# A mixture-of-experts tail: the first expert's weights fetched ahead of its rows, hooks regrouped, and branch bodies moved, on one Trainium2 core

## The chip, the core and the metric

One core of a Trainium2 chip runs the whole program. The metric is the device time of one launch in microseconds; lower is better.

## What is computed

The reference has three stages on 4608 tokens (8 batches of 576) with 512 features:

```python
attn = softmax(q @ k_p.T * scale) @ v_p
x = ((x @ w1) * (x @ w2)) @ w3 @ w_out
logits = x @ w_gate + modality_bias[modality_id]
e_idx = argmax(logits)
out = gate * (relu(x @ ew1[e_idx]) @ ew2[e_idx])
```

`k_p` and `v_p` are keys and values pooled by 8 along the sequence. `w1`, `w2` are 512x1024, `w3` is 1024x1024, `w_out` 1024x512. There are 8 experts of 512x1024 and 1024x512, and each token goes to one of them. With this data only two experts get tokens: one 2330, the other 2278.

## The kernel before

Every fp32 product of the heavy part is made of three matmuls of fp32r halves: high·high, high·low and low·high (`mm3`, lines 114 to 116). So each fp32 operand exists as a high half, written by ScalarE (ACT), and a low half, the difference, written by VectorE (DVE). In tile names `h` and `l` (`xh`, `xl`; `abh`, `abl`) stand for them.

The tokens go through attention and the first MLP in nine chunks of 512. In a chunk `mm1` runs eight blocks `m` (24 matmuls of 128x512 for a and b, whose product is split to `abh[m]`, `abl[m]`), and `mm_w` multiplies that with the folded `w3 @ w_out` in four tiles of 128 tokens (24 matmuls each). DVE then makes the gate's logits of each tile (line 579, eight reductions), `routing` (lines 585 to 603) the gate value and the one-hot choice `r_oh`, and `place` (lines 606 to 626) each token's place in its expert's list: two small matmuls on PE count tokens (`rps`, lines 610 and 611), twelve DVE operations make addresses, GpSimd (POOL) scatters the token numbers to `lst` in DRAM.

The last chunk and all expert work stand in `experts` (line 684). There the order of each engine is the written order (`manual_schedule`); side work is put between matmul blocks by *hooks*: lists of functions that run behind block `m` of `mm1` or `emm1`, or behind tile `i` of `mm_w`. An engine does its instructions in this order, so one that waits holds up all that stands behind it on that engine.

- **mm1 of the last chunk, hooks `h1`.** Behind block 2, `place_all` of chunk 7, `first_expert` (which expert has most tokens so far), `first_loads`, and `take_raw2`. `first_loads` reads the expert's number into an SP register, waits until the scatters are done (`settle`, line 629), fetches the first 512 token numbers (`fetch_ids`, 705), gathers their rows on POOL (`gather`, 709, into `xg`) and starts four loads of raw `w1` (713); `take_raw2` starts four of raw `w2`. The raw weights are split into halves by `w1p` and `w2p` (`piece`, 715: high on ACT in line 719, low on DVE in 720) behind blocks 5, 6 and 7.
- **Between mm1 and mm_w**, `turn` (737) copies the 16-bit halves of the gathered rows apart (742, 743) and transposes them by DMA on SP (744) into `xTu`. `join` (746), in two parts behind tile 1 of `mm_w`, puts them together again (752, 753) and splits them (`xh` 754 on ACT, `xl` 755 on DVE).
- **First group** (925): `emm1` is eight blocks of 12 matmuls on the 512 gathered tokens. Each block's result goes through ReLU to `hT` (763 on ACT, 764 on DVE). Its results take four PSUM banks in turn, so block 4 starts only when lines 763 and 764 of block 0 are done. Hooks: `routing` of the last chunk behind block 0, `place_all` behind 3, `plan` (lines 856 to 907, some 40 small DVE operations that make the table of all later groups) behind 4, the last two pieces of `w2` behind 6 and 7. Then `emm2`: per tile of 128 tokens 24 matmuls with `w2`, scale, and scatter to `out`.
- **Later groups** (`group`, 947): seven groups of four tiles, one of three, one of two. Each prefetches the next group's rows and weights, and splits its own `w2` pieces behind the blocks of `emm1`; the turn of the next rows comes behind block 6, the join behind an early tile of `emm2`.
- **Branches**: groups stand nested in `tc.If go{n}_{g}` (line 976), n = 0 for four tiles, 1 for three, and in the outer `tc.If` per kind (988); the two-tile kind has an if with an else (981). Every engine runs them by itself. With this data the three-tile chain ends after its first group, so `go1_0` is false. A false block waits for the engine's own instructions and branches to the code behind the if. In the program before, all seven bodies of the chain stand right behind their compares, the false blocks behind them, next to the outer if of the two-tile kind.

The ring and the split:

```python
def mm_ps(name, shape=(P, 512)):
    return psum.tile(list(shape), F32, name=name, tag="mm", bufs=4)

nc.scalar.copy(h2, r)
(sub or nc.vector).tensor_tensor(l2, r, h2.bitcast(F32), op=ALU.subtract)
```

Of the kernel before, what the change touches and what calls it, by code (L numbers as in the profile page):

```python
# [22 lines left out]
P = 128  # L23
# [66 lines left out]
def _program(outer, tc, nc, I, out):  # L90
# [16 lines left out]
    def st4(name, shape, dtype):  # L107
        return st.tile(list(shape), dtype, name=name, tag="st4", bufs=6)
# [519 lines left out]
    def settle(ent):  # L628
        nc.sync.dma_start(ent[0:1], I["pads"][0:4].rearrange("(o a) b -> o a b", o=1))
# [54 lines left out]
    def experts(x, old):  # L684
# [16 lines left out]
        def load_reg(ap, hi, engines=(ET.SP,)):  # L701
            return nc.values_load(ap, engines=list(engines), min_val=0, max_val=hi, skip_runtime_bounds_check_because="bounded by construction")
# [9 lines left out]
        def load_e(src, er, m2, raw):  # L712
            nc.sync.dma_start(raw, src[ds(er, P), 1024 * m2:1024 * m2 + 1024])
# [88 lines left out]

        def first_loads():
            first["e"], s0r = load_reg(t0i[0:1, 0:1], 896), load_reg(t0i[0:1, 1:2], LIST - CAP)
            settle(ents[-1])
            fetch_ids(s0r, 4)
            xg2 = [st4("xg", (P, 2, 512), F32) for i in range(2)]
            xg.extend(xg2[i // 2][:, i % 2] for i in range(4))
            gather(xg, 4, (NC_ - 1) * 512)
            first["raw"] = [st4("raw", (P, 1024), F32) for _ in range(4)]  # L810
            for m2 in range(4):
                load_e(I["ew1"], first["e"], m2, first["raw"][m2])

        raw2, xT = [], []

# [20 lines left out]
        w2p = lambda *ms: lambda: pieces(raw2, w2e, ms)  # L836
        for f in late_logits(ch - 1, old):
            f()
        h1 = {0: [lambda: r7.append(routing(ch - 1, lg))], 2: [lambda: place_all(r7[0]), first_expert, first_loads, take_raw2],
              5: [lambda: [take(m) for m in range(2, 6)], w1p(0, 1)], 6: [w1p(2, 3, 4, 5)], 7: [lambda: take(6), w1p(6, 7), w2p(0, 1, 2, 3)]}  # L840
        ab = mm1(ch, x, h1)

        xTu = w12.tile([P, 8, 512], U16, name="xTu", tag=w_tag(7), bufs=1)
        turn(xg, 4, nc.scalar.copy)
        xT.extend(xp.tile([P, 4, 512], F32R, name=n, tag=n) for n in ("xh", "xl"))
        x2s = []
        lo = lambda i, es=range(E): logits(ch, i, x2s, es)
        hw = {i: [lambda i=i: lo(i)] for i in range(4)}
        hw[0].insert(0, w2p(4, 5))
        hw[1] = [lambda: join(xT, 4, nc.scalar.copy, (0,)), lambda: lo(1, range(4)), lambda: join(xT, 4, nc.scalar.copy, (2,)), lambda: lo(1, range(4, 8))]  # L850
        mm_w(ch, ab, hw, W, x2s)

# [71 lines left out]

        def first_group():
            r8, nr = [], []
            hooks = {0: [lambda: r8.append(routing(ch, lg))], 3: [lambda: place_all(r8[0])], 4: [plan], 6: [w2p(6)], 7: [w2p(7)]}
            emm1(xT, hT, 4, hooks)
            er, sr = regs(0, 0)
            settle(ents[-1])  # L930
            fetch_ids(sr, 4)
            emm2(hT, 0)
            gather(xg, 4)
            loads1(er, (0, 1))
            nc.sync.dma_start(fence, xg[3][0:1, 0:1])
            loads1(er, (2, 3))
            loads2(er)
            emm2(hT, 1)
            pieces(raw1, w1e, (0, 1))
            emm2(hT, 2)  # L940
            transposes(xT, xg, 4)
            pieces(raw1, w1e, range(2, 8))
            emm2(hT, 3)
# [3 lines left out]
        def group(nxt, tiles, ntiles):  # L947
            nr = nxt()
            if nr:
                loads1(nr[0])  # L950
            hooks = {m: [lambda m=m: pieces(raw2, w2e, (m,))] for m in range(8)}
            if nr:
                hooks[6] += [lambda: turn(xg, ntiles, nc.vector.tensor_copy)]
                hooks[IDC_M] += [lambda: fetch_ids(nr[1], ntiles), lambda: gather(xg, ntiles)]
                hooks[7] += [lambda: loads2(nr[0])]
            emm1(xT, hT, tiles, hooks)
            half = (tiles + 1) // 2
            for i in range(tiles):
                emm2(hT, i)
                if nr:  # L960
                    if i == half - 1:
                        join(xT, ntiles, nc.vector.tensor_copy)
                    pieces(raw1, w1e, PIECES[tiles][i])

# [4 lines left out]
        def chain(n, g, tiles):  # L969

            if n < 2:
                if g < NG[n] - 2:
                    tc.mark_branch_hint_location(f"go{n}_{g}", counts[n] > g + 1, allE)
                group(lambda: regs(n, g + 1), tiles, tiles)
                if g < NG[n] - 2:
                    with tc.If(counts[n] > g + 1, label=f"go{n}_{g}"):  # L976
                        chain(n, g + 1, tiles)
            elif g == NG[n] - 2:
                group(lambda: None, tiles, tiles)
            else:  # L980
                with tc.If(counts[n] > g + 1) as more:  # L981
                    group(lambda: regs(n, g + 1), tiles, tiles)
                    chain(n, g + 1, tiles)
                with more.Else():
                    group(lambda: None, tiles, tiles)
# [51 lines left out]
```

## Time and profile before

| | |
|---|---|
| median of 3 runs | 1222.38 us (1221.27 to 1223.37) |
| the profiled execution's own time | 1223.66 us |
| span of its trace | 1221.6 us |
| mean granted TensorE clock | 0.983 |
| busy share of the span: PE, DVE, ACT, POOL | 95%, 66%, 41%, 26% |
| chunk 8's mm1 and mm_w end, first group begins | about 793 us |
| first group's emm1 / first tile of emm2 end | 822.4 / 827.85 us |
| three-tile group's last matmul starts | 1185.79 us |
| last matmul starts / last scatter starts | 1215.4 / 1216.9 us |

Times inside the trace count from the start of the span. In a timeline row the first number is the start, the second the duration, and in brackets stands the idle time of the engine just before and what ended it. Matmul rows overlap by design: an undisturbed 128x512 matmul is given as 0.39 us, but starts follow each other every 0.227 us (12 in 2.72 us), so gaps are measured between starts. `PEldq` is PE's own sequencer, where branches show. PEclk is the granted share of full clock.

### The profile page before, as it was taken

What the parts mean: (1) busy time and instruction counts of PE and PEld (TensorE: products, weight loads), DVE (VectorE), ACT (ScalarE), POOL (GpSimd) and SP (SyncE); (2) the same over time, 40 slices, a digit from 0 to 9 for tenths busy, and PEclk for the clock granted to TensorE, in tenths of its full rate; (3) what the DMA queues carried; (4) which work ended last, traced back from release to release, by engine and by line L of the source; (5) the groups of instructions that cost most, each with busy time, mean ns of one, the idle gap of its engine ahead of it and who ended that gap; (6) DMA issues with size and microseconds to landing.
All of it is one profiled execution on the core that took longest, in us unless ns stands there. A gap on an engine that the chain in (4) does not pass through costs nothing. (4 is left out here: it accounts for less than half of the span.)

```text
span 1221.6 us, 16215 instructions
## 1 busy us (share of the span) xinstructions
PE 1166.5 (95%) x5458; PEld 969.9 (79%) x5458; DVE 809.1 (66%) x1758; ACT 495.7 (41%) x967; POOL 313.5 (26%) x420
## 2 busy tenths in 40 slices
PE   4698899999999999999999999989999999999988
PEld 3466788888888888888888888868888888888867
DVE  6799787688687886877767684784444444445452
ACT  6587732222323223232232222713545545545452
POOL 3665501503315033150331101112121212122120
PEclk9899899999999999999999999989999999999998
DMA  9636332121121211211101000607645655654750
GB/s 334 205 139 221 133 114 72 48 76 43 57 91 48 73 45 56 91 48 71 47 18 36 1 35 17 217 10 266 182 129 182 192 144 172 208 156 131 203 149 18
DMA packets 89426, 136.68 MB, mean 112 GB/s; under 512 B 49304, under 2 KB 49560, under 8 KB 89176
## 3 DMA queue, kind: packets, MB, share of 16 engines
q1 hardware_dynamic: 82088, 115.72, 29.8%
q0 software_dynamic: 7232, 19.71, 5.0%
q8 instruction: 47, 0.77, 0.3%
q14 instruction: 59, 0.48, 0.1%
HBM read 106.26 MB, written 20.55 MB: 104 GB/s over the span
## 5 line engine op out<-in xcount | busy, mean ns | idle before, releaser
L114 PE MATMUL w<-xh,w 128*128 128x512 f32 x576 | 230.5, 400 | 3.7 <-ACT w L396 3.7
L116 PE MATMUL w<-xh,w 128*128 128x512 f32 x576 | 226.1, 392 | 1.4 <-POOL w L119 1.4
L115 PE MATMUL w<-xl,w 128*128 128x512 f32 x576 | 225.2, 391 | 0.0
L295 POOL TENSOR_TENSOR ex<-ex,sm 128x576 f32<-128x576 f32 x35 | 40.9, 1167 | 375.1 <-DVE sm L289 287.6
L114 PEld LDWEIGHTS w<-xh,w 128*128 128x128 f32 x576 | 108.9, 189 | 25.7 <-ACT w L396 4.1
L116 PEld LDWEIGHTS w<-xh,w 128*128 128x128 f32 x576 | 108.8, 189 | 25.8 <-POOL w L119 2.5
L115 PEld LDWEIGHTS w<-xl,w 128*128 128x128 f32 x576 | 109.0, 189 | 21.3
L764 DVE SCALAR_TENSOR_TENSOR abl<-e,abh 128x512 fp32r<-128x512 f32 (+2 forms) x80 | 51.8, 650 | 102.2 <-ACT abh L763 100.7
L114 PE MATMUL e<-e,abh 128*128 128x512 f32 x296 | 115.4, 390 | 0.5 <-ACT e L719 0.5
L115 PE MATMUL e<-e,abh 128*128 128x512 f32 x296 | 115.3, 390 | 0.2 <-DVE e L720 0.2
L116 PE MATMUL e<-e,abl 128*128 128x512 f32 x296 | 115.2, 389 | 0.0
L565 PE MATMUL x2ps<-Wh,abh 128*128 128x512 f32 x288 | 113.4, 394 | 0.8 <-DVE xl L324 0.8
L551 ACT CAST abh<-asb 128x512 fp32r<-128x512 f32 x72 | 44.7, 620 | 167.8 <-DVE asb L550 167.8
L565 PE MATMUL x2ps<-Wh,abl 128*128 128x512 f32 x288 | 112.4, 390 | 0.0
L565 PE MATMUL x2ps<-Wl,abh 128*128 128x512 f32 x288 | 112.3, 390 | 0.0
L777 POOL DMA_INDIRECT out<-o,idc x37 | 42.0, 1136 | 255.3 <-ACT o L776 143.0
L579 DVE CUSTOM_DVE_ANT_0 junk<-x2b,wgb,bias 128x512 f32<-128x512 f32 x144 | 102.3, 766 | 0.0
L579 DVE CUSTOM_DVE_ANT_0 junk<-x,wgb,bias 128x512 f32<-128x512 f32 x144 | 99.2, 755 | 0.2
L114 PE MATMUL e<-xh,e1h 128*128 128x512 f32 (+2 forms) x240 | 91.9, 383 | 5.6 <-DVEq L976 4.7
L550 DVE TENSOR_TENSOR asb<-asb,w 128x512 f32<-128x512 f32 x72 | 49.4, 685 | 66.2 <-PE w L116 31.1
L115 PE MATMUL e<-xl,e1h 128*128 128x512 f32 (+2 forms) x240 | 91.3, 380 | 0.0
L116 PE MATMUL e<-xh,e1l 128*128 128x512 f32 (+2 forms) x240 | 91.2, 380 | 0.0
(209 smaller groups left out, 2323.8 us busy)
## 6 DMA issues: line engine op xcount, KB each, us to landing
raw<-ew_in SPq DMA_DIRECT2D x80, 512.0 KB
q<-q_in SPq DMA_DIRECT2D x36, 256.0 KB
cv<-w_in SPq DMA_DIRECT2D x16, 512.0 KB
kr<-k_in SPq DMA_DIRECT2D x28, 288.0 KB
vr<-v_in SPq DMA_DIRECT2D x28, 256.0 KB
stage<-w_in SPq DMA_DIRECT2D x12, 512.0 KB
x2d<-x SPq DMA_DIRECT2D x18, 256.0 KB
x2d<-x2b SPq DMA_DIRECT2D x18, 256.0 KB
```

What stands on the lines that cost most here:

```text
L114: nc.tensor.matmul(ps, lhsT=wh, rhs=xh, start=start, stop=False)
L115: nc.tensor.matmul(ps, lhsT=wh, rhs=xl, start=False, stop=False)
L116: nc.tensor.matmul(ps, lhsT=wl, rhs=xh, start=False, stop=stop)
L295: eng.tensor_tensor(e3, e3, bc(sm.unsqueeze(2), [P, H, SP_]), op=ALU.mult)
L550: nc.vector.tensor_tensor(a, a, ps[1], op=ALU.mult)
L551: nc.scalar.copy(abh[:, m], a)
L565: nc.tensor.matmul(ps, lhsT=l[:, m, cols], rhs=r[:, m], start=m == 0 and r is Wh and l is abh, stop=m == 7 and l is abl)
L579: nc.vector.tensor_tensor_reduce(out=junk[e % 2], in0=x2s[i], in1=wgb[:, e], scale=1.0, scalar=bias[:, 4 * ch + i, e:e + 1], op0=ALU.mult, ...
L764: nc.vector.scalar_tensor_tensor(out=hT[1][:, m, :w], in0=ps[:, :w], scalar=0.0, in1=hT[0][:, m, :w].bitcast(F32), op0=ALU.max, op1=ALU.su ...
L777: nc.gpsimd.indirect_dma_start(out=out, out_offset=bass.IndirectOffsetOnAxis(idc[:, i, 0:1], 0), in_=o, in_offset=None, bounds_check=N - 1 ...
```

## The change

Five edits, all in `experts`. First, the eight raw weight loads are issued on SP ahead of `settle`, `fetch_ids` and the gather. Second, the pieces of the split stand in smaller groups behind blocks 4, 5, 6 and behind mm1; the low copy of the first `turn` goes from ACT to DVE. Third, in the first group `routing`, `place_all` and `plan` stand one block later, and the next gather ahead of the first `emm2`. Fourth, in groups of three and two tiles the turn stands behind block 7, and the three-tile group joins behind tile 0 instead of 1. Fifth, for n = 1 the body of `go1_g` is placed out of line, so that the false block follows the compare (for n = 0 nothing changes).

```diff
         def first_loads():
             first["e"], s0r = load_reg(t0i[0:1, 0:1], 896), load_reg(t0i[0:1, 1:2], LIST - CAP)
+            first["raw"] = [st4("raw", (P, 1024), F32) for _ in range(4)]
+            for m2 in range(4):
+                load_e(I["ew1"], first["e"], m2, first["raw"][m2])
+            take_raw2()
             settle(ents[-1])
             fetch_ids(s0r, 4)
             xg2 = [st4("xg", (P, 2, 512), F32) for i in range(2)]
             xg.extend(xg2[i // 2][:, i % 2] for i in range(4))
             gather(xg, 4, (NC_ - 1) * 512)
-            first["raw"] = [st4("raw", (P, 1024), F32) for _ in range(4)]
-            for m2 in range(4):
-                load_e(I["ew1"], first["e"], m2, first["raw"][m2])
...
-        h1 = {0: [lambda: r7.append(routing(ch - 1, lg))], 2: [lambda: place_all(r7[0]), first_expert, first_loads, take_raw2],
-              5: [lambda: [take(m) for m in range(2, 6)], w1p(0, 1)], 6: [w1p(2, 3, 4, 5)], 7: [lambda: take(6), w1p(6, 7), w2p(0, 1, 2, 3)]}
+        h1 = {0: [lambda: r7.append(routing(ch - 1, lg))], 2: [lambda: place_all(r7[0]), first_expert, first_loads],
+              4: [w1p(0, 1)], 5: [w1p(2, 3), lambda: [take(m) for m in range(2, 6)], w2p(0, 1)], 6: [w1p(4, 5), w2p(2, 3)]}
...
-        turn(xg, 4, nc.scalar.copy)
+        turn(xg, 4, nc.vector.tensor_copy)
+        take(6)
+        w1p(6, 7)()
+        w2p(4, 5)()
...
-        hw[0].insert(0, w2p(4, 5))
...
-            hooks = {0: [lambda: r8.append(routing(ch, lg))], 3: [lambda: place_all(r8[0])], 4: [plan], 6: [w2p(6)], 7: [w2p(7)]}
+            hooks = {1: [lambda: r8.append(routing(ch, lg))], 4: [lambda: place_all(r8[0])], 5: [plan], 6: [w2p(6)], 7: [w2p(7)]}
             emm1(xT, hT, 4, hooks)
             er, sr = regs(0, 0)
             settle(ents[-1])
             fetch_ids(sr, 4)
+            gather(xg, 4)
             emm2(hT, 0)
-            gather(xg, 4)
...
-                hooks[6] += [lambda: turn(xg, ntiles, nc.vector.tensor_copy)]
+                hooks[6 if tiles == 4 else 7] += [lambda: turn(xg, ntiles, nc.vector.tensor_copy)]
...
-            half = (tiles + 1) // 2
...
-                    if i == half - 1:
+                    if i == (tiles == 4):
                         join(xT, ntiles, nc.vector.tensor_copy)
...
-                    with tc.If(counts[n] > g + 1, label=f"go{n}_{g}"):
+                    with tc.If(counts[n] > g + 1, label=f"go{n}_{g}", preferred_fallthrough_block=n == 0):
                         chain(n, g + 1, tiles)
```

DVE in the first group's `emm1`, before (-) and after (+). `e_6932`, `e_6947`/`e_6963`, `e_6978`, `e_6994` and `e_7009` are the PSUM results of blocks 0 to 4; line 764 is the low half of the ReLU, lines 601 and 603 end `routing`, 614 begins the addresses of `place`.

```order
 L601 TENSOR_REDUCE r_mx<-r_d 128x4
 L603 TENSOR_TENSOR r_oh<-r_mx,c 128x32
-L764 SCALAR_TENSOR_TENSOR abl<-e_6963,abh 128x512
 L764 SCALAR_TENSOR_TENSOR abl<-e_6978,abh 128x512
 L767 TENSOR_SCALAR idc<-idn 128x8
 L764 SCALAR_TENSOR_TENSOR abl<-e_6994,abh 128x512
+L764 SCALAR_TENSOR_TENSOR abl<-e_7009,abh 128x512
 L614 TENSOR_TENSOR r_pos<-base,rps 128x8
```

Block 1's low half now stands ahead of `routing`, and block 4's ahead of the addresses; on PE the two `rps` matmuls stand behind block 4 instead of block 3.

ACT between mm1 and mm_w before: the last two of the eight turn copies, then the copies of `mm_w`'s tiles 0 and 1 (line 571) with two pieces of `w2` (`raw_6554`) between them, and the join.

```order
 L742 COPY pl<-xg 128x512
 L743 COPY pl<-xg 128x512
 L571 COPY x_6785<-x2ps 128x512
 L719 CAST e_6654<-raw_6554 128x512 x2
 L571 COPY x_6827<-x2ps 128x512
 L752 COPY xj<-xTu 128x1024
```

The same place after the change, from the last `abh` of mm1 on:

```order
 L551 CAST abh<-asb 128x512
 L742 COPY pl<-xg 128x512 x4
 L719 CAST e_6753<-raw 128x512 x2
 L719 CAST e_6662<-raw_6546 128x512 x2
 L571 COPY x_6789<-x2ps 128x512
 L571 COPY x_6827<-x2ps 128x512
 L752 COPY xj<-xTu 128x1024
```

Four copies of line 743 left ACT, and the pieces that stood ahead of the turn or behind tile 0 now stand between the turn and tile 0.

PE at the end of the three-tile chain, before: last matmul, the eight false blocks' jumps, the two-tile kind's outer if (988), its if with else (981), and a body.

```order
 L116 MATMUL e_12662<-e_6655,abl 128x512
 L976 UNCONDITIONAL_BRANCH x8
 L988 UNCONDITIONAL_BRANCH
 L988 COMPARE_AND_BRANCH
 L981 COMPARE_AND_BRANCH
 L114 MATMUL e_12704<-xh,e1h_6343 128x256
```

PE at the end of the first three-tile group after the change (line 978 is 976 of before):

```order
 L116 MATMUL e_10591<-e_6663,abl 128x512
 L978 COMPARE_AND_BRANCH
 L978 UNCONDITIONAL_BRANCH
 L975 REGISTER_ALU
 L1035 BRANCH_PREFETCH_HINT
 L114 MATMUL e_10647<-xh,e1h_6343 128x384
```

The false block of `go1_0` is now the row behind its compare; its unconditional branch leads to the two-tile kind's outer if, which stands about 1200 rows further on, behind the seven bodies.

## Rows read from the trace of the kernel before

**Rows 1.** Waits of PE, 640 to 1225 us: for what, us in total, times, longest

```profile
PE rps L610 <- DVE r_oh L603: 5.1, 1, 5.1
```

**Rows 2.** Timeline of PE, 796 to 815 us: start, duration, line, tile, [idle <-releaser]

```profile
803.75 0.39 PE L116 MATMUL e<-xh,e1l 128*128 128x512 f32 x1
...
809.25 0.21 PE L610 MATMUL rps<-r_oh,tri 128*128 128x32 bf16 x1 [5.11 <-DVE r_oh L603]
...
809.32 0.77 PE L114 MATMUL e<-xh,e1h 128*128 128x512 f32 x1
...
813.73 0.41 PE L115 MATMUL e<-xl,e1h 128*128 128x512 f32 x1
```

**Rows 3.** Busy time by stretch, 806.92 to 813.74 us: length, engines' busy us, PEclk

```profile
806.92:813.74 6.82, 4.49 (x13) 3.53 (x14) 5.33 (x25) 1.69 (x4) 0.43 (x1) 0.50 0.01 2
```

**Rows 4.** Timeline of PE, two gaps early in the run (columns as in 2)

```profile
26.91 0.80 PE L114 MATMUL wps<-f,f 128*128 128x512 f32 x1 [2.73 <-ACT f L396]
...
58.52 0.50 PE L114 MATMUL wps<-f,f 128*128 128x512 f32 x1 [1.24 <-ACT f L396]
```

**Rows 5.** Timeline of DVE, 781 to 827 us

```profile
781.28 1.29 DVE L720 TENSOR_TENSOR e<-raw,e 128x512 fp32r<-128x512 f32 x2 [3.99 <-ACT e L719]
...
788.26 1.23 DVE L755 TENSOR_TENSOR xl<-xj,xh 128x1024 fp32r<-128x1024 f32 x1 [0.24 <-ACT xh L754]
...
806.69 0.68 DVE L764 SCALAR_TENSOR_TENSOR abl<-e,abh 128x512 fp32r<-128x512 f32 x1
...
815.65 0.14 DVE L858 TENSOR_TENSOR r<-base,c 1x8 f32<-1x8 f32 x1
...
823.30 0.18 DVE L907 CAST ti<-rows 1x60 int32<-1x60 f32 x1
```

**Rows 6.** Timeline of ACT, 775 to 797 us

```profile
775.98 0.62 ACT L742 COPY pl<-xg 128x512 uint16<-128x512 uint16 x1
...
782.41 0.59 ACT L571 COPY x<-x2ps 128x512 f32<-128x512 f32 x1 [0.65 <-PE x2ps L565]
...
784.57 1.36 ACT L752 COPY xj<-xTu 128x1024 uint16<-128x1024 uint16 x1 [1.56 <-DMA xTu<-pl]
...
787.17 1.05 ACT L754 CAST xh<-xj 128x1024 fp32r<-128x1024 f32 x1
```

**Rows 7.** Lines 702, 705, 709, 748 to 776 us: xcount, ns min/median/max, first to last start

```profile
L702 SPq TENSOR_LOAD <-t0i x2: 281/386/492, 750.5 to 751.1; - x2
...
L705 SPq DMA_DIRECT2D idn<-lst x1: 448/448/448, 759.4 to 759.4; - x1
...
L709 POOL DMA_INDIRECT xg<-x2d,idn x4: 949/966/1442, 762.8 to 767.1; - x4
...
DMA to landing us min/median/max: 7.1/7.3/7.4
```

**Rows 8.** DMA view, 745 to 795 us: GB/s in 40 slices of 1.25 us

```profile
GB/s 0 0 0 7 1 1 1 1 0 0 0 0 26 154 269 397 357 410 416 423 403 397 400 413 161 0 45 186 192 196 201 374 64 0 0 0 0 0 195 97
```

**Rows 9.** Line 709, the later gather, 829 to 840 us

```profile
DMA to landing us min/median/max: 3.5/3.5/3.8
```

**Rows 10.** Timeline of PE, three-tile group, third emm2, 1172.8 to 1175 us

```profile
1172.90 0.39 PE L116 MATMUL e<-e,abl 128*128 128x512 f32 x1
...
1173.81 0.50 PE L114 MATMUL e<-e,abh 128*128 128x512 f32 x1 [0.52 <-ACT e L719]
...
1174.87 0.40 PE L116 MATMUL e<-e,abl 128*128 128x512 f32 x1
```

**Rows 11.** Timeline of PE, from the three-tile to the two-tile group

```profile
1185.79 0.39 PE L116 MATMUL e<-e,abl 128*128 128x512 f32 x1
...
1190.92 0.55 PE L114 MATMUL e<-xh,e1h 128*128 128x256 f32 x1 [4.74 <-DVEq L976]
```

**Rows 12.** Lines 976 and 981 on PE's sequencer, 1185 to 1188 us (as in 7)

```profile
L976 PEldq COMPARE_BRANCH  x1: 186/186/186, 1186.4 to 1186.4; - x1
...
L981 PEldq COMPARE_BRANCH  x1: 3577/3577/3577, 1186.7 to 1186.7; - x1
```

## The prediction

> **What bounds the kernel now.** I read the page's busy shares first (the table above): PE is busy for 95% of the span and the others are far behind, so what counts is where PE stands still or runs slowly, and the matmuls themselves don't change. Then PE's waits in the part that the change touches: one large wait for data, the placing of the last chunk's tokens behind the one-hot choice, 5.1 us [rows 1]. Apart from it there is a hole at the exit of the three-tile chain [rows 11] and a small one inside that chain's group [rows 10]. Each is a term below; everywhere else in this part PE's matmuls start every 0.227 us, and edits there can only do harm.
>
> **Hole 1, the first group.** The last matmul of block 3 starts at 803.75, so block 4 could start at 803.98. PE first has the two `rps` matmuls, which come at 809.25, and the next ten matmuls, 809.32 to 813.73, run at half clock [rows 2]: the granted clock of that stretch is 0.50, 1.2 instead of 2.4 GHz [rows 3]. They take 4.41 us, where ten take 2.27. So the hole costs 809.32 - 803.98 = 5.34, and the clock 2.14: 7.48 us. Why so late? DVE made logits without a break until block 0's low half at 806.69, and only then `routing`, since the first join's `xl` at 788.26 [rows 5].
>
> *What the edits do there.* `place_all` goes behind block 4, so PE no longer waits for it. But block 4 uses block 0's PSUM bank, and must wait for block 0's low half, which stands behind the same logits: that is late next. Before, it ends at 806.69 + 0.68 = 807.37 [rows 5]. Can DVE come there earlier? Its chain now begins when the pieces and four turn copies are done; ACT is rid of four turn copies, and DVE's stall of 3.99 us for ACT's pieces [rows 5] goes. The first logits can start before 780. This gain is not all kept, because the first `xl` waits for ACT's join, and ACT's join now stands behind its copy of tile 1, which PE releases at 782.41 [rows 6]. That copy needs some 0.5 us, so the join can start at 782.93 instead of 784.57 [rows 6], and `xl` and all behind it come 1.64 us earlier: block 0's low half ends at 805.73. PE starts block 4 at about 805.8, 1.8 us late, and has to do the two `rps` matmuls behind it (0.07, from 809.25 to 809.32). Does the clock fall? The nearest gaps in this trace: 1.24 us idle was followed by a matmul of ordinary length (0.50), 2.73 us idle by one of 0.80 [rows 4], like the 0.77 at half clock [rows 2]. Here PE would idle 1.6 to 1.7; that is nearer to 1.24, so I take no fall and keep 2.14 us as the other end. Gain: 7.48 - 1.8 - 0.07 = 5.6.
>
> *What is late next.* `plan` goes from behind block 4 to behind block 5, on DVE 7.8 us (815.65 to 823.48 [rows 5]), and the low halves of blocks 6 and 7 and the last `w2` pieces stand behind it. Block 5 now ends at 805.8 + 24 x 0.227 + 0.07 = 811.3; `plan` started 1.45 us after the end of block 4 (814.2, [rows 2, 5]), so now 812.8, ending at 820.5. Two low halves and two pieces at some 0.6 each (1.29 for a pair of pieces [rows 5]) end at 822.9. `emm2` tile 0 starts at 811.3 + 5.44 = 816.8, and its last three matmuls, 21 x 0.227 later at 821.5, need them: they wait 1.4 us. Before, DVE was ahead of `emm2` here. Kept: 5.6 - 1.4 = **4.2 us** at the end of tile 0.
>
> *What hides the moved gathers.* (a) First gather: SP has the expert's number at 751.1 + 0.5, and then stood in `settle` until `fetch_ids` at 759.4 [rows 7]. The eight raw loads are issued in that time now, from about 751.6 on, instead of behind it. `fetch_ids` itself is not moved, since `settle` holds it until the scatters are done; but its 4 KB stand behind the raws on SP's queue. Eight raws are 4.2 MB, which at 400 GB/s [rows 8] take 10.5 us, and the stream began about 1.5 us behind its first issue (760 to 761.5, the first full slices [rows 8]): until about 763.6. The gathers began 3.4 us after `fetch_ids`; from an arrival behind the raws I take 766.2 for the first (762.8 before) and 770.5 for the last (767.1). They took 7.3 us to land beside the raws [rows 7]; alone a gather takes 3.5 [rows 9], so the last lands at 774.0, against 774.4 before. The turn can start on ACT right behind mm1's last split, where ACT had pieces ahead of it before, some 3 us earlier: about 772.9. From the turn's first copy to the join were 8.6 us (775.98 to 784.57 [rows 6]): 781.5 here, under the 782.93 that tile 1 sets anyway. The cover is some 1.5 us. (b) The next gather, now ahead of tile 0's `emm2`, no longer waits for that tile's scatter on POOL. With `plan` done 3.0 us earlier and no scatter ahead, it starts about as much earlier as PE needs it. (c) The pieces of `w1` and `w2` in blocks 4 to 6 stand in idle time of ACT and DVE. I cost (b) and (c) at nothing.
>
> **Hole 2, the three-tile group.** At 1173.81 PE waits for the last `w2` piece, which stood behind the turn of hook 6. From 1172.90 to 1174.87 are three starts, 1.97 us where 0.68 would do [rows 10]: **1.3 us**. The turn now stands behind that piece, and so the gain is all of it. The join goes one tile earlier, in a stretch where DVE and ACT wait for PE; nothing.
>
> **Hole 3, the exit of the three-tile chain.** Before: the last matmul ends at 1186.18, the first of the two-tile group starts at 1190.92 [rows 11]. In it PE's sequencer spends 0.19 on the near jump and 3.58 on the far one into the else [rows 12]; the jump out of the compare of `go1_0` was taken while PE's queued matmuls still ran, and cost nothing. Now the compare falls through, but the false block ends in an unconditional jump 1200 rows away. That one stands behind the wait for PE's own last matmul, so it can't run ahead. If it costs what the other far jump costs, PE spends 3.58 twice: the jump starts at 1186.22 and ends at 1189.8, the outer if follows, the far jump into the else ends at about 1193.5, and the matmuls start at 1193.9: **3.0 us later**. The change moves a hidden fetch into the open. No row shows an unconditional far jump alone; the bounds are 0.19, the near jump (then the exit costs what it cost), and 3.58 on top of everything (+3.6). I take the far one, as its distance is of the same order as that of the row with 3.58, and the near jump's is a few instructions. The Trainium skill speaks for both: "Runtime: NRT & Kernel Launch", section "Instruction fetch mechanics", says that a taken branch to a place outside the two pages at hand has to fetch the target by DMA first, and the trace agrees for the far jump of 3.58. By this rule the change loses 3.0 us here. After the hole PE ran at half clock before, and I let it cost the same.
>
> **Sum**, against the profiled execution: -4.2 - 1.3 + 3.0 = -2.5, so 1223.66 - 2.5 = 1221.2. That execution was 1.3 us above the median of the three runs; for the median, 1222.38 - 2.5 = **1219.9**. A measurement of this kernel can tell about 0.2%, 2.4 us, from no change: below 1219.9 is faster, above 1224.8 slower. The forecast lies at the edge.
>
> **Rivals.** *The jump is cheap.* If the target is fetched while PE waits for its matmuls, it costs 0.19 like the near jump, hole 3 stays as it is, and the sum is -5.5: 1216.9. For it: the wait for the matmuls leaves time for a fetch. Against it: the far jump into the else was not fetched ahead either. 17%. (The Trainium skill's "Advanced Engine Details and Errata", section "Control Flow Timing", gives about 51 ns for a branch-always; by that the result would be 0.14 us lower still. The 3.58 us of [rows 12] show that a branch here can be far from such figures.)
>
> *The rows come late (slower).* The token numbers stand behind the raws on SP's queue, so a slow stream of raws delays the gathers, the turn, the join, all of DVE's logits and block 0's low half. Up to 775.5 for the last landing the cover holds; from there each us is a us at block 4, and as soon as PE idles there for nearly 3 us the clock falls and takes 2.1 more. The sum is above zero from about 777 on. With the landing at 780: 1.8 + 4.5 = 6.3 of waiting at block 4 and 2.1 of clock take back 6.6, and the total is +4.1: 1226.5. For it: the stream with the raws in it lasted 14 us before [rows 8]. Against it: they start some 8 us earlier, without the gathers beside them. 15%.
>
> *The change does less than it says (same).* DVE's chain is not earlier, or the shorter wait at block 4 drops the clock all the same: 2.1 us of hole 1 come back, -0.4, 1222.0. For it: 1.7 us lies between the two gaps that I have, and 1.64 of DVE's gain rests on one copy. 18%.
>
> **Chances and range.** Forecast 50%, its own range 1218.3 to 1221.5 (a cheaper or dearer jump by 0.6, 1 us in hole 1). About half of it is under 1219.9. With the cheap jump: faster 0.47; same, from the other half and the third rival, 0.37; slower 0.16. The range has to take in the cheap jump and the third rival, and reaches a little into the second: 1215.9 to 1223.6.
>
> **What would show it.** Right: PE waits under 2 us before block 4 with a DVE low half as releaser and keeps full clock behind it; some 1.4 us of waits in `emm2` tile 0 for `plan`'s followers; no wait in the third `emm2` of the three-tile group; and some 7.7 us between the last three-tile matmul and the first two-tile one, with two branches of over 2 us on PE's sequencer. Wrong: a clock of 0.5 behind block 3, an exit hole of under 5 us, or a first join that waits for the transposes.

## The result

The changed kernel is slower: 1229.51 us median (1227.63 to 1230.98, six runs) against 1222.86, a ratio of 1.0055 with a 95% interval of 1.0042 to 1.0068. A second measurement, beside two of the experiments, gave 1227.06 and 1.0035 (1.0022 to 1.0049). The forecast was 1219.9. One run of experiment 3, of 1684.85 us, stands apart from all others and is in no ratio. The profiled execution took 1229.55 us with a span of 1227.5, against 1223.66 and 1221.6 before.

PE's waits of the changed kernel, from 640 us to the end (for what, us in total, times, longest):

```profile
PE e L114 <- issue: 9.2, 1, 9.2
PE e L114 <- DVE abl L764: 4.4, 1, 4.4
PE e L114 <- ACTq L978: 1.0, 1, 1.0
PE e L115 <- DVE xl L755: 0.9, 1, 0.9
PE e L115 <- DVE e L720: 0.7, 2, 0.5
```

The wait for `rps` of [rows 1] is gone, as forecast. In its place stands one of 4.4 us for block 0's low half (764), where 1.6 to 1.7 were forecast, and a new largest one at the exit, 9.2 us, in which PE waited for nothing that the profile shows (`issue`); its sequencer was busy with two branches, below. PE's timeline shows a late start of the first group, then the last matmul of block 3 and the first of block 4, then the last of the three-tile and the first of the two-tile group (behind the first group, line numbers are two or three higher than before):

```profile
796.24 0.50 PE L115 MATMUL e<-xl,e1h 128*128 128x512 f32 x1 [0.94 <-DVE xl L755]
...
805.48 0.39 PE L116 MATMUL e<-xh,e1l 128*128 128x512 f32 x1
...
810.30 0.80 PE L114 MATMUL e<-xh,e1h 128*128 128x512 f32 x1 [4.44 <-DVE abl L764]
...
1187.48 0.39 PE L116 MATMUL e<-e,abl 128*128 128x512 f32 x1
...
1197.12 0.55 PE L114 MATMUL e<-xh,e1h 128*128 128x256 f32 x1 [9.25 <-issue]
```

Set beside the same matmuls of before [rows 2, 11], PE stands as follows in the two traces:

| matmul | before | changed | difference |
|---|---|---|---|
| last of the first group's block 3 | 803.75 | 805.48 | +1.7 |
| first of block 4 | 809.32 | 810.30 | +1.0 |
| first of `emm2`'s tile 1 | 827.85 | 830.76 | +2.9 |
| last of the three-tile group | 1185.79 | 1187.48 | +1.7 |
| first of the two-tile group | 1190.92 | 1197.12 | +6.2 |
| last of all | 1215.43 | 1221.35 | +5.9 |

Of the +1.7 at block 3, 1.1 are PE's wait for the join's `xl` (1.33 us between two starts instead of 0.23), and 0.6 are stretched starts in `mm_w`'s first tile, right behind the last halves of `mm1` (776.1 to 777.2). The step from +2.9 to +1.7 is the three-tile group, as forecast. In these two profiles the first group loses 2.9 where 4.2 us of gain were forecast, and the exit loses 4.5 where 3.0 were.

**The first group.** The same lines as in [rows 7], after:

```profile
L629 SPq DMA_DIRECT2D r_ent<-pads_in x1: 300/300/300, 765.0 to 765.0; - x1
...
L705 SPq DMA_DIRECT2D idn<-lst x1: 419/419/419, 765.5 to 765.5; - x1
...
L709 POOL DMA_INDIRECT xg<-x2d,idn x4: 949/972/1273, 773.8 to 777.9; - x4
...
DMA to landing us min/median/max: 3.6/4.5/5.3
```

`settle` ends at 765.0, not 758.8, so the token numbers are asked for 6.1 us later (765.5, before 759.4). They then take 8.3 us until the first gather (773.8) instead of 3.4. The last gather starts at 777.9 and lands some 4 us later: the turn's wait for the last row tile ends at 782.2, against 774.4 for the landing before. The stream of the raws from 745 in slices of 1.25 us as in [rows 8], first the busy share of the DMA engines in tenths, then GB/s:

```profile
DMA  0000008998658999979961004766899999300000
GB/s 0 0 0 7 1 1 170 220 76 23 29 69 272 404 413 367 75 203 377 394 238 37 0 7 82 203 177 187 233 180 183 201 186 346 133 0 0 0 0 0
```

The first raws run from 752.5, at 170 and 220 GB/s; then, from 755 to 760, the whole core moves only 76, 23, 29 and 69 GB/s, with its DMA engines busy for 0.5 to 0.9 of the time, and the rest of the raws comes from 760 to 771. That is the stretch in which the four scatters of `place` were under way. Their rows, before and then changed:

```profile
L623 POOL DMA_INDIRECT lst<-r_ent,r_dst x4: 958/962/969, 749.0 to 752.8; - x4
...
DMA to landing us min/median/max: 4.3/5.9/6.2
...
L623 POOL DMA_INDIRECT lst<-r_ent,r_dst x4: 957/960/970, 748.9 to 752.7; - x4
...
DMA to landing us min/median/max: 6.2/7.0/12.1
```

They are issued at the same time, and the slowest takes 12.1 us instead of 6.2 to land; `settle` waits for it. The token numbers come behind the last raw. On DVE (low copy of the turn, first `xl`, low half of blocks 0 and 1) and on ACT (the join):

```profile
780.73 0.43 DVE L743 COPY pl<-xg 128x512 uint16<-128x512 uint16 x1 [2.86 <-DMA xg<-x2d,idn]
...
787.34 1.36 ACT L752 COPY xj<-xTu 128x1024 uint16<-128x1024 uint16 x1 [1.51 <-DMA xTu<-pl]
...
791.13 1.23 DVE L755 TENSOR_TENSOR xl<-xj,xh 128x1024 fp32r<-128x1024 f32 x1
...
809.55 1.29 DVE L764 SCALAR_TENSOR_TENSOR abl<-e,abh 128x512 fp32r<-128x512 f32 x2
```

The turn stands still for 2.9 us for the rows, the join waits for the transposes behind it and starts at 787.34 instead of 784.57 [rows 6], `xl` comes at 791.13 instead of 788.26 [rows 5], and block 0's low half at 809.55 instead of 806.69. PE idles for 4.4 us, and the clock falls as it did before (granted clock of the stretch behind block 3, then of the one behind the exit):

```profile
809.03:815.85 6.82, 5.55 (x15) 4.08 (x15) 4.43 (x16) 1.22 (x4) 0.00 (x0) 0.50 0.01 2
...
1191.32:1201.56 10.24, 4.44 (x21) 4.47 (x22) 0.75 (x2) 1.00 (x2) 0.98 (x1) 0.50 0.12 19
```

**The exit.** On PE's sequencer, the false block's jump and the jump into the else, as in [rows 12] (the profile names both kinds of branch alike):

```profile
L978 PEldq COMPARE_BRANCH  x1: 3726/3726/3726, 1188.1 to 1188.1; - x1
...
L983 PEldq COMPARE_BRANCH  x1: 4972/4972/4972, 1192.0 to 1192.0; - x1
```

Both are far now, one behind the other, and the second takes 4.97 us, longer than the 3.58 that it took alone.

### The profile page after: what moved, and what is told of

Its sections match the earlier page's. It is cut to its first block, busy times and chain, and to the rows that moved or that the text cites. A ratio compares the mean times of both kernels' runs of the same rounds, so it can differ in the third digit from the quotient of the medians.

```text
span 1227.5 us, 16220 instructions
## 1 busy us (share of the span) xinstructions
PE 1168.9 (95%) x5458; PEld 969.9 (79%) x5458; DVE 811.1 (66%) x1762; ACT 495.3 (40%) x963; POOL 314.8 (26%) x420
## 4 chain that ended last, share of the span: by engine, by line
PE 74%; DVE 10%; DMA 8%; issue 3%; ACT 2%; POOL 2%; SPq 0%; another core or an unknown queue 0%; POOLq 0%; DVEq 0%; ACTq 0%
PE x2ps L565 13%; PE w L114 10%; PE w L116 9%; PE w L115 9%; PE e L115 8%; PE e L114 8%; PE e L116 8%; DMA xg<-x2d,idn 4%; PE sc L265 3%; DVE junk L579 2%; DMA out<-o,idc 2%; DVE scr L394 2%; DVE scr L395 2%; DMA raw<-ew_in 1%; PE atp L304 1%
## 5 line engine op out<-in xcount | busy, mean ns | idle before, releaser
L763 ACT ACTIVATE abh<-e 128x512 fp32r<-128x512 f32 (+2 forms) x80 | 45.2, 566 | 119.1 <-PE e L116 109.9
```

The lines of the kernel that those rows point to most:

```text
L763: nc.scalar.activation(hT[0][:, m, :w], ps[:, :w], AF.Relu)
```

## The experiments

Each gives its median beside that of the kernel before, measured with it on the same chip, then the ratio of the runs (not that of the medians) with its 95% interval.

**1. The exit alone**, on the kernel before.

```diff
-                    with tc.If(counts[n] > g + 1, label=f"go{n}_{g}"):
+                    with tc.If(counts[n] > g + 1, label=f"go{n}_{g}", preferred_fallthrough_block=n == 0):
```

> The kernel before with the fifth edit alone (go1 bodies out of line). Theory: the false block's unconditional jump and the far jump into the else both stand behind PE's last matmul and are fetched one after the other. Then the gap between the last matmul of the three-tile group and the first of the two-tile group grows from 5.1 us (start to start) to about 9.6, as in the changed kernel, with two branches of 3.5 us or more on PE's sequencer, and the time to about 1227 us (+4 to +4.5). Rival: most of the longer gap in the changed kernel comes from its later turn or from fetches of other edits; then this kernel is under 1224.5 us.

1225.92 against 1222.06 us, 1.0031 (1.0020 to 1.0041): +3.9. The gap is 9.1 us from start to start, and the sequencer shows the same two branches:

```profile
L976 PEldq COMPARE_BRANCH  x1: 3257/3257/3257, 1183.8 to 1183.8; - x1
...
L981 PEldq COMPARE_BRANCH  x1: 4932/4932/4932, 1187.3 to 1187.3; - x1
```

**2. The exit with one far jump**, on the kernel of experiment 1. The else now follows its compare.

```diff
-                with tc.If(counts[n] > g + 1) as more:
+                with tc.If(counts[n] > g + 1, preferred_fallthrough_block=False) as more:
```

> The kernel before with the fifth edit, and the two-tile group's else now placed right behind its compare. This takes away the second of the two far jumps. Theory: two fetches stand in series at the changed exit (3.3 and 4.9 us); with one, the gap of 9.1 us falls to about 5 (PE's jump 3.3 and DVE's, which ends some 5.2 us behind PE's last matmul), and the time to about that of the kernel before, 1221.5 to 1223, unless the jump behind the else now shows at the end of the run (up to +3). Rival: the time at the exit is not set by the jumps' fetches but by the joined engines (DVE or ACT late); then the gap stays over 8 us.

1223.26 against 1222.72, 1.0006 (0.9997 to 1.0015). The gap fell from 9.1 to 4.6 us:

```profile
L976 PEldq COMPARE_BRANCH  x1: 3577/3577/3577, 1184.8 to 1184.8; - x1
...
L981 PEldq COMPARE_BRANCH  x1: 67/67/67, 1188.6 to 1188.6; - x1
```

One far jump of 3.58 is left, the branch into the else is 0.07. So the two far jumps in series made the loss of experiment 1, and no waiting engine did. The exit is 0.5 us shorter than before and the end of the run, from PE's last matmul, 1.0 longer (7.2 against 6.2): nothing is won. The body of the else now ends in a far jump of its own:

```profile
L981 PEldq COMPARE_BRANCH  x1: 3340/3340/3340, 1209.3 to 1209.3; - x1
```

It takes 3.34 us, but PE's queued matmuls run on without a gap until the last one at 1213.18: a far jump that is taken while the engine has work queued costs PE nothing here.

**3. The changed kernel without its exit**, measured twice, the second time beside the changed kernel, and once with the numbers first.

```diff
-                    with tc.If(counts[n] > g + 1, label=f"go{n}_{g}", preferred_fallthrough_block=n == 0):
+                    with tc.If(counts[n] > g + 1, label=f"go{n}_{g}"):
```

> The changed kernel without its fifth edit (go1 as before). If the parts add up, the time falls by what the exit alone cost (3.8 us, 2.4 to 5.0): about 1225.5 us, 3 us above the kernel before, all of it from the first group, with a gap of 4.4 to 5 us ahead of block 4 and 5 to 5.5 us at the exit. If the long exit of the changed kernel is also due to its other edits, more comes back: 1224 us or less.

1221.96 against 1222.72, 1.0001 (0.9990 to 1.0012): 7.5 us under the changed kernel's first median, which did not fit the 3.9 of experiment 1. So both ran once more, side by side:

> The changed kernel once more, beside the next two on the same chip. If the exit costs 4 us and the rest of the 7.5 us between the changed kernel and the one without its fifth edit is scatter of the clock's state in the first group, the median is 1226 to 1228 here. If it is 1229 or more again, the exit costs more beside the other edits than alone.

> The changed kernel without its fifth edit, once more. Additive parts: 4 us under the changed kernel of the same call. Not additive: 6.5 us or more under it, and 1222 us again.

1227.06 and 1223.15 against 1222.13. The difference is 3.9, as in experiment 1. The rest of the 7.5 did not come back; the same changed kernel stood at 1229.51 first and at 1227.06 now, and I put it down to scatter between the measurements. Without the exit, the changed kernel can't be told from the kernel before (1.0001, and 1.0005 with 0.9996 to 1.0014).

> The changed kernel with settle and the token numbers ahead of the raw loads, and without its fifth edit. With the exit at 4 us: 1222.5 us, 4 under the run with the numbers first and the changed exit (1226.5); with the exit at 7.5: 1219 us.

1223.73 against 1222.13, 1.0009 (1.0000 to 1.0018); 2.8 under the run with the changed exit (next). The exit costs 3 to 4 us.

**4. Token numbers first**, the changed kernel with this order on SP:

```diff
+            settle(ents[-1])
+            fetch_ids(s0r, 4)
             first["raw"] = [st4("raw", (P, 1024), F32) for _ in range(4)]
...
             take_raw2()
-            settle(ents[-1])
-            fetch_ids(s0r, 4)
```

> The changed kernel with settle and the fetch of the token numbers put back ahead of the eight raw loads on SP (everything else as changed). Theory: in the changed kernel the raw loads slow the four scatters that settle waits for (done at 758.7 before, 764.8 changed), and the token numbers stand behind the raws (2 us before, 7 us changed). Then settle ends near 758.8 again, the numbers are there near 761.5, the gathers begin near 763 and have landed by 775, and the low half of block 0 is over 2 us earlier than the 810.1 of the changed kernel; but the raws come late for the pieces that stand behind blocks 4 and 5, and ACT may wait for them by 1 to 3 us. Time 1223 to 1227 us. Rival: the regrouped pieces (ACT and DVE late at the turn) make the loss of the first group; then it stays and the time is 1228.5 us or more.

1226.49 against 1222.06, 1.0034 (1.0021 to 1.0047). PE's waits:

```profile
PE e L114 <- issue: 8.7, 1, 8.7
PE e L114 <- DVE abl L764: 3.0, 1, 3.0
PE x2ps L565 <- ACT asb L549: 1.4, 1, 1.4
PE x2ps L565 <- ACT abh L551: 0.9, 1, 0.9
```

The wait for block 0 is down to 3.0 us and the clock stayed at 1.00 behind it. But now ACT waits for raws with the pieces of blocks 4 to 6, and its copies for mm1 behind them: PE waits 2.3 us in the first tile of `mm_w`. With the exit's 3 to 4 us taken off, the changed first group wins nothing in this order either.

**5. Settle first, numbers behind the raws**: the changed kernel with `settle` alone put back ahead of the raws.

> The changed kernel with settle alone put back ahead of the raw loads; the fetch of the token numbers stays behind them. This tells the two delays apart. If the slowed scatters are what counts, the numbers are there by about 766 and the first group gains some 5 us at the gathers. If the order on SP's queue counts, settle ends near 758.8 but the numbers land only when the raws are through, near 772, the last rows land at about 780 as in the changed kernel, and the time stays within 1.5 us of 1229.5. I expect the second.

1229.68 against 1222.06, 1.0054 (1.0040 to 1.0068), as the changed kernel.

```profile
L629 SPq DMA_DIRECT2D r_ent<-pads_in x1: 294/294/294, 756.3 to 756.3; - x1
...
L705 SPq DMA_DIRECT2D idn<-lst x1: 461/461/461, 762.2 to 762.2; - x1
...
L709 POOL DMA_INDIRECT xg<-x2d,idn x4: 946/968/1022, 772.6 to 776.4; - x4
...
DMA to landing us min/median/max: 3.3/5.2/7.4
```

```profile
GB/s 0 0 7 1 1 1 1 0 0 0 128 210 360 341 292 419 419 419 423 333 21 7 0 121 151 197 255 109 117 124 113 288 99 118 249 170 0 0 0 0
```

`settle` is done at 756.3 and the raws, now behind the scatters, run without a break, at 292 to 423 GB/s behind the first two slices. Still the numbers, asked for at 762.2, need until 772.6 for the first gather: they come when the raws are through. The order on SP's queue alone is enough for the late rows.

**6. Half of the raws ahead**: the changed kernel with the four raws of `w2` behind the numbers.

> The changed kernel with only the four raw w1 loads ahead of settle and the token numbers, the four of w2 behind them. Theory: 2.1 MB instead of 4.2 MB stand ahead of the numbers, so these land soon after settle; settle itself ends late only by what four raws slow the scatters, 759 to 762. Gathers begin at 763 to 766 beside the w2 raws and have landed by 773 to 777. The first group loses little or nothing against the kernel before, and with the exit (+4) and the three-tile group (-1) the time is 1224 to 1226.5 us. Rival: any raw ahead of the scatters holds them up as eight do (settle at 764 or later); then 1228 us or more.

1227.16 against 1222.34, 1.0034 (1.0021 to 1.0047).

```profile
L629 SPq DMA_DIRECT2D r_ent<-pads_in x1: 298/298/298, 763.7 to 763.7; - x1
...
L705 SPq DMA_DIRECT2D idn<-lst x1: 419/419/419, 764.2 to 764.2; - x1
...
L709 POOL DMA_INDIRECT xg<-x2d,idn x4: 946/966/1031, 767.5 to 771.3; - x4
...
DMA to landing us min/median/max: 4.7/5.6/6.4
```

```profile
GB/s 0 0 0 7 1 1 151 236 76 29 43 131 285 410 298 20 39 174 315 403 374 416 413 367 33 0 13 45 165 190 195 184 346 134 0 0 0 0 0 100
```

The rival was right on `settle`: 763.7 with four raws, nearly as late as with eight, and the same hole in the stream (76, 29, 43 GB/s). SP was through with issuing its four raws at 754.0 and then waited for the scatters, so `settle` is held by them and not by the time that SP takes to issue loads (eight raws kept SP until 761.1 in the changed kernel). The numbers then took only 3.3 us to the first gather. So there are two delays: raws beside the scatters, and numbers behind the raws.

**7. Raws ahead alone**, on the kernel before.

> The kernel before with the first edit alone (raw loads ahead of settle, fetch and gather). Theory: the rows land near 782 instead of 774.4, as in the changed kernel; the turn, still eight copies on ACT, ends near 783, the first join starts some 3 to 4 us later than 784.6, and all of DVE's logits and the one-hot choice with it: PE waits 8 to 9 us instead of 5.1 ahead of rps, 1225 to 1226.5 us. Rival: the late rows are hidden under ACT's and DVE's other work, since the pieces are done earlier; then within 1 us of 1222.1.

1224.43 against 1222.34, 1.0016 (1.0007 to 1.0025). `settle` was reached at 764.1 here. The wait ahead of `rps` grew from 5.1 to 6.3 us: late rows cost 2.1 us, less than expected: ACT copied each row tile as it landed, so the turn's last copy ended at 781.9 instead of 780.2, not at 783, and the join began at 785.3.

**8. The later hooks alone**, on the kernel before.

```diff
-            hooks = {0: [lambda: r8.append(routing(ch, lg))], 3: [lambda: place_all(r8[0])], 4: [plan], 6: [w2p(6)], 7: [w2p(7)]}
+            hooks = {1: [lambda: r8.append(routing(ch, lg))], 4: [lambda: place_all(r8[0])], 5: [plan], 6: [w2p(6)], 7: [w2p(7)]}
```

> The kernel before with the third edit's hooks alone (routing behind block 1, place behind 4, plan behind 5; the gather stays). Theory: PE now waits before block 4 for block 0's low half, which DVE ends at 807.4 as before; so PE starts block 4 at 807.45 instead of 809.32, a gap of 3.5 us. If the clock falls behind a gap of 3.5, the first group gains 1.8 and loses 1.4 for the pieces behind plan: 1222.5 us; if it doesn't, 1220.3. Rival: block 4 waits for nothing but place, and the hole disappears: 1217 us.

1221.36 against 1222.06, 0.9995 (0.9985 to 1.0004): no difference that can be told. PE waits 3.46 us, as worked out:

```profile
807.32 0.50 PE L114 MATMUL e<-xh,e1h 128*128 128x512 f32 x1 [3.46 <-DVE abl L764]
...
808.97 0.63 PE L114 MATMUL e<-xh,e1h 128*128 128x512 f32 x1
```

Block 4 waits for block 0's low half; moving `place` alone only changes what PE waits for. The first matmul behind the gap has its ordinary length, but the clock falls a little later (0.63 for a matmul at 808.97).

**9. The late turn alone**, on the kernel before (fourth edit).

> The kernel before with the fourth edit alone (turn behind block 7 and join behind tile 0 in the three-tile group). Theory: the wait for the last w2 piece, 1.3 us, is gone and nothing takes its place: 1220.8 us, which is within what can be told from 1222.1; in the trace no wait of PE between 1172 and 1175. Rival: the later turn delays the join or the rows of the two-tile group, which then starts later behind the exit; then the same time or more.

1222.24 against 1222.34, 1.0000 (0.9991 to 1.0008). PE's wait in the three-tile group is gone from the trace; in its place the exit's gap is 0.3 us longer (5.47 from start to start, 5.13 before), and what is left, 1.0, is below what can be told. All runs with this edit and the old exit have the longer gap, 5.47 to 5.80, and those without it 5.10 to 5.15.

**10. First group without raws ahead**, on the kernel before.

```diff
-        turn(xg, 4, nc.scalar.copy)
+        turn(xg, 4, nc.vector.tensor_copy)
+        w2p(4, 5)()
...
-        hw[0].insert(0, w2p(4, 5))
```

and the third and fourth edits.

> The kernel before with the third and fourth edits, and of the second only the first turn's low copies on DVE, with the two pieces of w2 that stood behind tile 0 now right behind the turn. The raw loads stay behind the token numbers, go1 stays as before. This is the prediction's first group without the two parts that failed. Theory: the first join starts behind ACT's copy of tile 1, block 0's low half ends 1.6 us earlier than before, PE idles 1.6 to 1.9 us ahead of block 4 and keeps its clock; the first group gains about 4 us, the three-tile group about 1: 1217 us. Rival: the gain of DVE's chain is eaten (the join waits for something else, or the clock falls behind a gap under 2 us); then 1219.5 to 1221 us.

1222.26 against 1222.34, 0.9998 (0.9989 to 1.0007). The expected 1217 did not come: PE still idles 4.0 us ahead of block 4. On ACT:

```profile
774.31 2.18 ACT L742 COPY pl<-xg 128x512 uint16<-128x512 uint16 x4
...
783.59 1.35 ACT L752 COPY xj<-xTu 128x1024 uint16<-128x1024 uint16 x1 [2.26 <-DMA xTu<-pl]
```

The turn begins where it began, behind six pieces, so the transposes end no earlier, and the join waits for them (2.26 us) and not for tile 1's copy: counted from the first matmul of `mm_w` it starts at 13.9 us, 13.2 before. Making the turn shorter does nothing; it would have to begin earlier. So the next run moves it.

**11. The turn ahead of the pieces**, on the kernel before, raws and exit as there, with the third and fourth edits.

```diff
-              5: [lambda: [take(m) for m in range(2, 6)], w1p(0, 1)], 6: [w1p(2, 3, 4, 5)], 7: [lambda: take(6), w1p(6, 7), w2p(0, 1, 2, 3)]}
+              5: [lambda: [take(m) for m in range(2, 6)], w1p(0, 1)], 6: [w1p(2, 3, 4, 5)], 7: [lambda: take(6)]}
...
-        turn(xg, 4, nc.scalar.copy)
+        turn(xg, 4, nc.vector.tensor_copy)
+        w1p(6, 7)()
+        w2p(0, 1, 2, 3, 4, 5)()
...
-        hw[0].insert(0, w2p(4, 5))
```

> The kernel before with the third and fourth edits, and the first turn (low copies on DVE) straight behind mm1, ahead of the pieces of hook 7, which now follow it; raw loads and exit as before. This gives the turn the early start that the prediction counted on, without raw loads ahead. Theory: the first transpose is issued about 3 us earlier than before; the join is then held by ACT's copy of tile 1 and starts 1.6 us earlier, block 0's low half 1.6 us earlier, PE idles about 1.8 us ahead of block 4 and keeps its clock: 1217 us. Rival: as in the run without raws and exit, the gap ahead of block 4 stays at 3.5 us or more, because the last transposes or the pieces behind the turn (ACT to 779, DVE to 780) hold the join or the logits; then 1221 to 1222.5 us.

1218.13 against 1222.72, 0.9966 (0.9954 to 0.9978): by this ratio 4.2 us faster than the kernel before, and the best of all. ACT and PE:

```profile
771.89 2.18 ACT L742 COPY pl<-xg 128x512 uint16<-128x512 uint16 x4
...
781.46 0.59 ACT L571 COPY x<-x2ps 128x512 f32<-128x512 f32 x1 [2.73 <-PE x2ps L565]
781.94 1.36 ACT L752 COPY xj<-xTu 128x1024 uint16<-128x1024 uint16 x1
```

```profile
802.79 0.39 PE L116 MATMUL e<-xh,e1l 128*128 128x512 f32 x1
...
804.79 0.50 PE L114 MATMUL e<-xh,e1h 128*128 128x512 f32 x1 [1.61 <-DVE abl L764]
...
805.13 0.39 PE L115 MATMUL e<-xl,e1h 128*128 128x512 f32 x1
```

The turn starts right behind mm1, the join right behind tile 1's copy with no wait for the transposes, and PE idles 1.61 us. Counted from the first matmul of `mm_w`, the first one of `emm2`'s tile 1 comes 4.1 us earlier than before (52.4 for 56.5). The granted clock behind the wait (803 to 810 us, third number from the end):

```profile
803.00:810.00 7.00, 5.39 (x25) 4.16 (x25) 6.33 (x24) 1.80 (x4) 0.00 (x0) 1.00 0.01 2
```

## Why the prediction was wrong

Both signs that were to show it wrong came: a clock of 0.50 behind block 3, and a first join that waits for the transposes. Between the forecast of -2.5 us and the two profiles (+5.9 at the last matmul) lie 8.4 us; 7.1 of them are the first group, 1.5 the exit.

- *"`fetch_ids` itself is not moved, since `settle` holds it until the scatters are done".* This step failed. It took the end of the scatters as fixed, while the raws were to run just beside them. `settle` moved by 6.2 us (765.0 for 758.8), since the slowest scatter took 12.1 us to land; experiments 6 and 7 show it again with half the raws (763.7) and without the other edits (764.1), experiment 5 that it goes when the raws come behind the scatters (756.3).
- *"Eight raws ... until about 763.6 ... I take 766.2 for the first".* The numbers did stand behind the raws, which was priced, but with the raws at 400 GB/s from their start. Measured, the stream ended near 771 and the first gather came at 773.8. Experiment 5, with an undisturbed stream, has 772.6 all the same, since the raws then start 5 us later. The rival "the rows come late" was the right mechanism, with the landing at 782 instead of 780; it got 15% because it was priced on the stream alone. Its price was too dear: with each us of landing a us at block 4, that block would have started at 812.3, and it started at 810.30; from the last landing to the join it counted 7.5 us (774.0 to 781.5), and 5.2 were measured (782.15 to 787.34). That its 1226.5 lies close to the second measurement, 1227.06, is in part luck: its landing was too early and its exit too cheap, and its price of a late landing too dear.
- *"Gain: 5.6".* The mechanism held, the place for it did not. With an early turn (experiment 11) the wait is 1.61 us, where 1.6 to 1.7 were forecast, the clock stays, and the first group is 4.1 us shorter in the trace, where 4.2 were forecast; the kernel gains 4.2 us in all, where the first group and the three-tile group were to give 5.5. The prediction's view that a shorter turn and an earlier chain follow from the edits needed rows and pieces in time; in the changed kernel the rows were late, in experiment 4 the raws, and in experiment 10, with both in time, the turn still stood behind the pieces.
- *The pieces in idle time, costed at nothing.* Wrong with late raws: 2.3 us of PE in experiment 4. Their cover was the landing of the raws, which the prediction didn't name. In the changed kernel itself ACT stood still for 4.7 us for raws, ahead of 768.49; its last high half of `mm1` came 3.1 us later than before (775.46, 772.33), and the 0.6 us of stretched starts on PE stand right behind it.
- *"emm2 tile 0 ... wait 1.4 us".* Right in kind: PE's two waits for the low halves of pieces there are 0.7 us in the profile's measure, 1.0 from start to start. Some 0.6 of the +1.9 us between block 4 and tile 1 is the clock: it was at half for 6.82 us in both profiles, but less of that fell into PE's idle time.
- *Three-tile group, -1.3.* Seen in the trace (+2.9 to +1.7), but alone nothing that can be measured, as the exit grows by 0.3 us or more (experiment 9).
- *Exit, +3.0.* Right in kind, too small: +3.9 alone. That is above the +3.6 which the prediction took as its upper bound. The undersized term is the second jump, taken at 3.58 and measured at 4.93 and 4.97. The Trainium skill, "Runtime: NRT & Kernel Launch", section "Instruction fetch mechanics", says that a taken branch to a place outside the two pages at hand waits for a fetch of its target. Experiments 1 and 2 agree with it: 3.26 and 4.93 us for the two far jumps, 0.07 for the branch whose target follows it.
- *The chances.* They don't follow from their parts: half of the forecast's 50% and the cheap jump's 17% are 0.42 for faster, not 0.47.

The sum: the exit costs 3.9 us by itself. Without it the changed kernel is level with the kernel before (experiment 3), so the first and the three-tile group together won nothing where 5.5 us were forecast. Of the 6.6 us of the first measurement 2.7 are left beside the exit, of the 4.9 of the second 1.0; no experiment shows these as a loss of the first group, though the profile of the changed kernel has 2.9 there.

## What to carry to other kernels

A load that is pulled ahead is ahead of everything that follows on its queue, and beside everything that is already under way; ask for both who waits behind it, and which small transfer it will run beside. Where a step gates a chain (here the turn), move that step ahead of the work that is not urgent, rather than bringing the inputs of that work earlier. Keep an exit that is taken at one far jump, and let that be taken while the engine still has work queued (3.34 us hidden in experiment 2).

## What the runs showed of the hardware

- Raw loads of 512 KB beside four indirect scatters of token numbers slowed each other: 23 to 76 GB/s for 5 us, against 292 to 423 GB/s when the scatters were done, and the slowest scatter landed in 12.1 us instead of 6.2, `settle` 5 to 6 us later. With half the loads it was the same (10.7 us). What in the DMA engines does this was not settled.
- A far jump right behind another one took 4.59 to 4.97 us on PE in the six profiles that have one, the first of the two 3.26 to 4.31, a single one that PE waited for 3.46 to 3.92. Why the second is longer no run shows.
- PE's clock after a gap is not decided by the gap's length alone. It stayed at 1.00 behind 1.61 us idle (experiment 11) and behind 3.05 in the first group of experiment 4, and fell to 0.50 behind 3.04 in the same first group of its twin without the exit, and behind 3.3, 3.5, 4.0, 4.4 and 5.1 us, for 3.4 us in some profiles and 6.8 in others. The length of the first matmul behind the gap, by which the prediction read the clock, doesn't tell it: behind 3.04, 3.3, 3.5 and 4.0 us it was an ordinary 0.50, and the clock fell within 1.3 us. So one profile of such a kernel says little about 2 us.
